# Forgetting attention and an expert layer: feeding the second stage group by group

## The chip, the cores and the metric

The kernel runs on one core of a Trainium2 chip. The core has a matrix engine (TensorE, shown as PE, with its weight loads as PEld), three engines for elementwise work (VectorE, shown as DVE; ScalarE, shown as ACT; GpSimd, shown as POOL) and a queue engine (SyncE, SP). Each works through its own instructions in a fixed order. Data moves between memory and the on-chip buffer by DMA; transfers are issued from SP, ACT and POOL and share 16 DMA engines. Matmul results land in PSUM, which has eight banks of 512 fp32 columns. The metric is the device time of the program in microseconds (us).

## The reference

Inputs: q, k, v of shape (8 batches, 8 heads, 576 positions, 64), forget gates f (8, 8, 576), and two weight matrices (512 x 2048 and 2048 x 512), all fp32.

```python
scores = (q @ k^T) / sqrt(64) + cum[..., :, None] - cum[..., None, :]   # cum = cumsum(log f)
scores = where(causal, -1e9, scores)          # a position sees itself and earlier ones
attn = softmax(scores)
x = (attn @ v)            # rearranged to (8*576 tokens, 512)
h = x @ w_in              # 4608 x 2048
out = (h - tanh(h)) @ w_out   # 4608 x 512
```

## The kernel before

A *group* is one batch entry: 8 heads of 576 positions. The 64 heads are one loop. `emit_group_dma` loads a group on POOL's queue, and `emit_group_transpose` turns q and k on PE (72 transposes of 128 columns) into QT and KT.

`emit_qk` makes the scores of a head, transposed: five tiles of up to 128 keys by the positions that see them (576, 448, 320, 192 and 64 wide). A tile is one matmul (two for the first, L172 and L174, since it is wider than a bank), an addition of the causal mask on its diagonal block by DVE (L179) and the exponential on ACT (L183). Tile 0 has a PSUM tile of its own of two banks (`ps_q0`), the others share two banks (`ps_qk`). The sum over keys needs no extra work: the values carry a column of ones, so `emit_av` gives 64 rows of weighted values and one row of sums in one PSUM tile (L199, L201). ACT copies that to `ot` (L207); SP sends the row of sums to `rsgt` (L208), and POOL sends the values, cast to fp16, into `xT` (L209), which holds x transposed: 4 blocks of 128 features (two heads each) by 4608 tokens.

`emit_group_finish` divides by the sums. DVE takes the reciprocal of a group's 8 rows (L214), ACT sends them to memory (L215), and then for each of 4 pairs of heads ACT's queue loads a broadcast `bcp`: one row to 64 partitions, the next to the other 64 (L218). DVE multiplies the block of `xT` with it (L221). `bcp` has 2 buffers.

The expert layer (MoE in the names) works in 9 units of 512 tokens. `emit_moe1` makes 16 pieces of the hidden layer: 4 matmuls (`hps`, L258), tanh on ACT (`th`, L262), the sum on DVE (`gt`, L265). `emit_moe2` makes 4 output tiles from 16 matmuls each (`ops`, L271), copied by ACT (`ost`, L274) and stored by SP (L276). A unit needs all four blocks of `xT` for its tokens, so unit u needs groups up to that of its last token: u for units 0 to 7, and group 7 for unit 8.

The order on each engine is drawn up when the program is built, by a planner of the Tile framework: it takes instructions by their place in the source as a priority, among those whose inputs and buffers are free by its own estimate of the times. So an instruction far down in the source may stand early in an engine's queue. In the source all eight `emit_group_finish` stand behind the head loop, then the attention's buffers are given back, then come the MoE's buffers, the weight loads and the units. A waiting instruction holds all behind it on its engine.

Of the kernel before, what the change touches and what calls it, by code (L numbers as in the profile page):

```python
# [1 line left out]

# [5 lines left out]
FP32 = mybir.dt.float32  # L9
BF16 = mybir.dt.bfloat16  # L10
FP16 = mybir.dt.float16
AF = mybir.ActivationFunctionType
ALU = mybir.AluOpType
# [5 lines left out]
def kernel(  # L19
# [10 lines left out]
    nc = tc.nc  # L30
    P = 128

    B, H, S, D = q.shape
    NH = B * H
    DM, DFF = moe_w_in.shape
# [3 lines left out]
    NJB = (S + P - 1) // P  # L39
# [3 lines left out]
    qscale = float(D) ** -0.5  # L43
    inv_qscale = float(D) ** 0.5
    NFT = DFF // P
    NCH = DM // P
    UW = 512
    NU = NT // UW
# [10 lines left out]
    qkt = tc.alloc_tile_pool(name="qkt", bufs=2)  # L59
    stg = tc.alloc_tile_pool(name="stg", bufs=2)  # L60
    vpl = tc.alloc_tile_pool(name="vpl", bufs=2 * H)
    aex = tc.alloc_tile_pool(name="aex", bufs=3 * NJB)
    fin = tc.alloc_tile_pool(name="fin", bufs=4)
    ps_tr = tc.alloc_tile_pool(name="ps_tr", bufs=2, space=bass.MemoryType.PSUM)
    ps_q0 = tc.alloc_tile_pool(name="ps_q0", bufs=1, space=bass.MemoryType.PSUM)
    ps_qk = tc.alloc_tile_pool(name="ps_qk", bufs=2, space=bass.MemoryType.PSUM)
    ps_av = tc.alloc_tile_pool(name="ps_av", bufs=1, space=bass.MemoryType.PSUM)

    xT = xtp.tile([P, NCH, NT], FP16)
    win = moe.tile([P, NCH, DFF], FP16)  # L70
    wout = moe.tile([P, NFT, DM], FP16)
# [20 lines left out]
    while sft < S:  # L92
        nc.vector.tensor_copy(out=dst[0:NH, 0:sft], in_=src[0:NH, 0:sft])
        nc.vector.tensor_tensor(out=dst[0:NH, sft:S], in0=src[0:NH, sft:S],
                                in1=src[0:NH, 0:S - sft], op=ALU.add)
# [9 lines left out]
    biasT = cst.tile([P, NJB, NH], FP32)  # L105
    for t in range(NJB):
        jn = JSZ[t]
# [5 lines left out]
    QTs, KTs, VAs, VTs, AEX, OTP, RSG, BCP = {}, {}, {}, {}, {}, {}, {}, {}  # L113
    rsdram = nc.dram_tensor("fox_rowsum", (NH, S), FP32).ap()
    rcdram = nc.dram_tensor("fox_rrowsum", (NH, S), FP32).ap()
# [43 lines left out]
    def emit_qk(h: int):  # L159
        g, hl = divmod(h, H)  # L160
        QT, KT = QTs[g], KTs[g]
        for t in range(NJB):
            j0 = t * P
            jn = JSZ[t]
            wid = S - j0
            if t == 0:
                ps = ps_q0.tile([P, 1024], FP32, tag="qk0")
            else:
                ps = ps_qk.tile([P, 512], FP32, tag="qk")
            lhsT = KT[0:D + 1, hl * S + j0: hl * S + j0 + jn]  # L170
            if t == 0:
                nc.tensor.matmul(out=ps[0:jn, 0:512],  # L172
                                 lhsT=lhsT, rhs=QT[0:D + 1, hl * S: hl * S + 512])
                nc.tensor.matmul(out=ps[0:jn, 512:S],  # L174
                                 lhsT=lhsT, rhs=QT[0:D + 1, hl * S + 512: hl * S + S])
            else:
                nc.tensor.matmul(out=ps[0:jn, 0:wid],  # L177
                                 lhsT=lhsT, rhs=QT[0:D + 1, hl * S + j0: hl * S + S])
            nc.vector.tensor_tensor(out=ps[0:jn, 0:jn], in0=ps[0:jn, 0:jn],  # L179
                                    in1=tri[0:jn, 0:jn], op=ALU.add)  # L180
            ae = aex.tile([P, S], FP16, tag="ae")
            AEX[(h, t)] = ae
            nc.scalar.activation(out=ae[0:jn, j0:S], in_=ps[0:jn, 0:wid], func=AF.Exp,  # L183
                                 bias=biasT[0:jn, t, h:h + 1], scale=qscale)

    def emit_av(h: int):
        g, hl = divmod(h, H)
        c = hl // 2
        upper = hl % 2
        assert H // 2 <= 4  # L190
        avp = ps_av.tile([P, 1024], FP32, tag="av")
        for t in range(NJB):
            j0 = t * P
            jn = JSZ[t]
            lhsT = (VTs[g][0:jn, hl, 0:D + 1] if t == NJB - 1
                    else VAs[h][0:jn, t, 0:D + 1])
            ae = AEX.pop((h, t))
            if j0 < 512:
                nc.tensor.matmul(out=avp[0:D + 1, j0:512], lhsT=lhsT, rhs=ae[0:jn, j0:512],  # L199
                                 start=(t == 0), stop=(t == NJB - 2))  # L200
            nc.tensor.matmul(out=avp[0:D + 1, 512:S], lhsT=lhsT, rhs=ae[0:jn, 512:S],  # L201
                             start=(t == 0), stop=(t == NJB - 1))
        m = H * S // P
        if hl == 0:
            RSG[g] = fin.tile([P, S], FP32, tag="rsg", name="rsgt")
        ot = fin.tile([P, S], FP32, tag="ot", bufs=6)
        nc.scalar.activation(out=ot[0:D + 1, :], in_=avp[0:D + 1, 0:S], func=AF.Copy)  # L207
        nc.sync.dma_start(out=RSG[g][hl:hl + 1, :], in_=ot[D:D + 1, 0:S])  # L208
        nc.gpsimd.dma_start(out=xT[upper * D:(upper + 1) * D, c, g * S:(g + 1) * S],  # L209
                            in_=ot[0:D, :])  # L210

    def emit_group_finish(g: int):
        rsg = RSG.pop(g)
        nc.vector.reciprocal(out=rsg[0:H, :], in_=rsg[0:H, :])  # L214
        nc.scalar.dma_start(out=rcdram[g * H:(g + 1) * H, :], in_=rsg[0:H, :])  # L215
        for c in range(H // 2):
            bcp = fin.tile([P, S], FP32, tag="bcp", bufs=2)
            nc.scalar.dma_start(  # L218
                out=bcp,
                in_=bass.AP(rcdram.tensor, (g * H + 2 * c) * S, [[S, 2], [0, D], [1, S]]))  # L220
            nc.vector.tensor_tensor(out=xT[:, c, g * S:(g + 1) * S],  # L221
                                    in0=xT[:, c, g * S:(g + 1) * S], in1=bcp, op=ALU.mult)

    pending = {}
    for hh in range(NH + 1):
        g, hl = divmod(hh, H)
        if hh == 0:
            pending[0] = emit_group_dma(0)
            emit_group_transpose(0, *pending.pop(0))
        if hh < NH:  # L230
            if hl == 1 and g + 1 < B:
                pending[g + 1] = emit_group_dma(g + 1)
            if hl == H - 2 and g + 1 < B:
                emit_group_transpose(g + 1, *pending.pop(g + 1))
            emit_qk(hh)
        if 1 <= hh <= NH:
            emit_av(hh - 1)
    for g in range(B):
        emit_group_finish(g)

    for p in (ps_av, ps_qk, ps_q0, ps_tr, fin, aex, vpl, stg, qkt):
        p.release()

    gtp = tc.alloc_tile_pool(name="gtp", bufs=2 * NFT)
    tmp = tc.alloc_tile_pool(name="tmp", bufs=2)
    ps_m1 = tc.alloc_tile_pool(name="ps_m1", bufs=2, space=bass.MemoryType.PSUM)
    ps_m2 = tc.alloc_tile_pool(name="ps_m2", bufs=2, space=bass.MemoryType.PSUM)

    nc.gpsimd.dma_start(out=win, in_=moe_w_in.rearrange("(c p) f -> p c f", p=P))
    nc.gpsimd.dma_start(out=wout, in_=moe_w_out.rearrange("(t p) e -> p t e", p=P))  # L250

    GT = {}

    def emit_moe1(u: int):
        for ft in range(NFT):
            hps = ps_m1.tile([P, UW], FP32, tag="m1")
            for ci in range(NCH):
                nc.tensor.matmul(out=hps, lhsT=win[:, ci, ft * P:(ft + 1) * P],  # L258
                                 rhs=xT[:, ci, u * UW:(u + 1) * UW],
                                 start=(ci == 0), stop=(ci == NCH - 1))  # L260
            th = tmp.tile([P, UW], FP32, tag="th")
            nc.scalar.activation(out=th, in_=hps, func=AF.Tanh, scale=-1.0)  # L262
            gt = gtp.tile([P, UW], FP16, tag="gt")
            GT[(u, ft)] = gt
            nc.vector.tensor_tensor(out=gt, in0=hps, in1=th, op=ALU.add)  # L265

    def emit_moe2(u: int):
        for m in range(UW // P):
            ops = ps_m2.tile([P, DM], FP32, tag="m2")
            for ft in range(NFT):  # L270
                nc.tensor.matmul(out=ops, lhsT=GT[(u, ft)][:, m * P:(m + 1) * P],  # L271
                                 rhs=wout[:, ft, :], start=(ft == 0), stop=(ft == NFT - 1))
            ost = tmp.tile([P, DM], FP32, tag="ost")
            nc.scalar.activation(out=ost, in_=ops, func=AF.Copy)  # L274
            r0 = u * UW + m * P
            nc.sync.dma_start(out=out[r0:r0 + P, :], in_=ost)  # L276

    for u in range(NU + 1):
        if u < NU:
            emit_moe1(u)  # L280
        if u > 0:
            emit_moe2(u - 1)

    for p in (ps_m2, ps_m1, tmp, gtp):
        p.release()


# [28 lines left out]
```

## Time and profile before

| | before |
|---|---|
| median of 6 runs | 700.12 us (699.83 to 700.81) |
| the profiled execution | 699.83 us, span 698.1 us |
| mean granted TensorE clock | 0.726 |
| instructions | 7647 |

The span runs from the first to the last instruction. Busy times count an engine's own work, without waits and without issuing DMAs. The clock is given as a share of full speed, 2.4 GHz; 0.50 is 1.2 GHz.

### The profile page before, as it was taken

How to read it: one execution, taken by the hardware profiler on the slowest of the kernel's cores; microseconds unless marked ns; L12 is line 12 of the kernel's file. 1: busy time of each engine (PE TensorE's matmuls, PEld its weight loads, DVE VectorE, ACT ScalarE, POOL GpSimd, SP SyncE). 2: the span in 40 equal slices, each digit the busy share in tenths (PEclk: the TensorE clock that was granted, in tenths of full speed). 3: DMA queues.
4: the chain of work that ended last, by engine and by line, in shares of the span. 5: the costliest groups of instructions: out<-in, count | busy, mean ns of one | idle time of the engine just before them, and what ended most of it. 6: DMA issues, size and time to landing. Idle time of an engine off the chain costs nothing.

```text
span 698.1 us, 7647 instructions
## 1 busy us (share of the span) xinstructions
PE 531.4 (76%) x2693; PEld 277.5 (40%) x2693; DVE 283.5 (41%) x611; ACT 291.0 (42%) x567; POOL 127.4 (18%) x244
## 2 busy tenths in 40 slices
PE   2899626465866757867845646299999999999997
PEld 1566313333443434534423322034444444444443
DVE  6547322514524624624624234244533524425330
ACT  1558422344444435444544532144433534434331
POOL 6647502332332332222001000000000000000000
PEclk9759655555555555555565558589999999999999
DMA  9999993993494594334111220100011010010111
GB/s 98 104 103 93 117 166 52 151 110 57 42 113 68 48 97 67 31 52 67 15 51 40 45 55 23 46 31 31 15 46 45 31 46 30 31 62 15 46 46 76
DMA packets 131479, 42.97 MB, mean 62 GB/s; under 512 B 115888, under 2 KB 122096, under 8 KB 131440
## 3 DMA queue, kind: packets, MB, share of 16 engines
q0 software_dynamic: 119712, 23.08, 43.3%
q1 hardware_dynamic: 7440, 9.81, 3.9%
q10 hardware_dynamic: 4288, 9.59, 3.9%
q8 instruction: 21, 0.34, 0.2%
q14 instruction: 18, 0.15, 0.1%
HBM read 46.28 MB, written 9.58 MB: 80 GB/s over the span
## 4 chain that ended last, share of the span: by engine, by line
PE 39%; DMA 14%; DVE 3%; ACT 2%; issue 1%; DVEq 0%; ACTq 0%
PE hps L258 18%; PE ops L271 17%; DMA bcp<-fox_rrowsum 13%; DVE rsgt L214 2%; PE ps L177 1%; ACT ae L183 1%; PE avp L199 1%; DVE ps L179 1%; PE tq L150 0%; PE tk L155 0%; PE ps L172 0%; DVE xT L221 0%; ACT ot L207 0%; PE avp L201 0%; DMA xT<-ot 0%
## 5 line engine op out<-in xcount | busy, mean ns | idle before, releaser
L183 ACT ACTIVATE ae<-ps,biasT 128x576 f16<-128x576 f32 (+4 forms) x320 | 148.8, 521 | 215.1 <-DVE ps L179 214.5
L258 PE MATMUL hps<-xT,win 128*128 128x512 f16 x576 | 143.3, 390 | 23.4 <-DVE gt L265 23.4
L177 PE MATMUL ps<-QT,KT 65*128 65x448 bf16 (+3 forms) x256 | 86.1, 387 | 97.1 <-ACT ae L183 95.1
L265 DVE TENSOR_TENSOR gt<-hps,th 128x512 f16<-128x512 f32 x144 | 99.2, 690 | 131.2 <-ACT th L262 131.2
L271 PE MATMUL ops<-wout,gt 128*128 128x512 f16 x576 | 138.2, 382 | 0.0
L262 ACT ACTIVATE th<-hps 128x512 f32<-128x512 f32 x144 | 86.0, 597 | 108.0 <-PE hps L258 94.8
L179 DVE TENSOR_TENSOR ps<-ps,tri 128x128 f32<-128x128 f32 (+1 forms) x320 | 79.4, 278 | 89.9 <-PE ps L177 54.7
L199 PE MATMUL avp<-ae,va 128*65 128x512 f16 (+3 forms) x256 | 98.3, 435 | 8.8 <-ACT ot L207 7.5
L258 PEld LDWEIGHTS <-win 128*128 128x128 f16 x576 | 56.6, 99 | 99.2 <-issue 41.2
L221 DVE TENSOR_TENSOR xT<-xT,bcp 128x576 f16<-128x576 f16 x32 | 24.3, 759 | 151.6 <-DMA bcp<-fox_rrowsum 147.8
L271 PEld LDWEIGHTS <-gt 128*128 128x128 f16 x576 | 56.7, 98 | 69.3 <-issue 2.2
L177 PEld LDWEIGHTS <-KT 65*128 65x128 bf16 (+1 forms) x256 | 32.1, 132 | 126.9 <-issue 123.7
L209 POOL DMA_DIRECT2D xT<-ot x64 | 34.2, 535 | 164.1 <-ACT ot L207 156.2
L133 POOL DMA_DIRECT2D va<-in_v_dram x64 | 49.7, 779 | 56.5 <-issue 39.1
L201 PE MATMUL avp<-ae,va 128*65 128x64 f16 x256 | 58.8, 248 | 0.0
L155 PE MATMUL tk<-idbf,ksb 128*65 128x128 bf16 x288 | 44.6, 291 | 14.3 <-DVE KT L157 9.0
L199 PEld LDWEIGHTS <-va 128*65 128x65 f16 x256 | 40.4, 158 | 31.8 <-issue 23.1
L274 ACT ACTIVATE ost<-ops 128x512 f32<-128x512 f32 x36 | 21.4, 596 | 66.8 <-PE ops L271 66.8
L201 PEld LDWEIGHTS <-va 128*65 128x65 f16 x256 | 40.4, 158 | 17.7 <-issue 15.2
L150 PE MATMUL tq<-idbf,qsb 128*64 128x128 bf16 x288 | 42.2, 293 | 5.7 <-DVE QT L152 4.4
L207 ACT ACTIVATE ot<-avp 65x576 f32<-65x576 f32 x64 | 41.1, 642 | 11.9 <-PE avp L201 11.9
L155 PEld LDWEIGHTS <-ksb 128*65 128x65 bf16 x288 | 31.1, 156 | 25.6 <-issue 15.9
(40 smaller groups left out, 267.7 us busy)
## 6 DMA issues: line engine op xcount, KB each, us to landing
bcp<-fox_rrowsum ACTq DMA_DIRECT2D x32, 288.0 KB
out_dram<-ost SPq DMA_DIRECT2D x36, 256.0 KB
qsb<-in_q_dram POOLq DMA_DIRECT2D x8, 576.0 KB, 7.6
ksb<-in_k_dram POOLq DMA_DIRECT2D x8, 576.0 KB, 10.5
xT<-ot POOLq DMA_DIRECT2D x64, 72.0 KB, 4.8
va<-in_v_dram POOLq DMA_DIRECT2D x64, 64.0 KB, 6.0
win<-in_moe_w_in_dram POOLq DMA_DIRECT2D x1, 2048.0 KB, 39.3
wout<-in_moe_w_out_dram POOLq DMA_DIRECT2D x1, 2048.0 KB, 15.9
```

Of the source, the lines that this page charges most:

```text
L133: nc.gpsimd.dma_start(out=va[:, :, 0:D], in_=vf[g * H + hl, 0:JTOP, :].rearrange("(n p) d -> p n d", p=P))
L150: nc.tensor.transpose(out=tq[0:D, t * P:(t + 1) * P], in_=qsb[:, c0 + t, :], identity=idbf)
L155: nc.tensor.transpose(out=tk[0:D + 1, t * P:(t + 1) * P], in_=ksb[:, c0 + t, :], identity=idbf)
L177: nc.tensor.matmul(out=ps[0:jn, 0:wid], lhsT=lhsT, rhs=QT[0:D + 1, hl * S + j0: hl * S + S])
L179: nc.vector.tensor_tensor(out=ps[0:jn, 0:jn], in0=ps[0:jn, 0:jn], in1=tri[0:jn, 0:jn], op=ALU.add)
L183: nc.scalar.activation(out=ae[0:jn, j0:S], in_=ps[0:jn, 0:wid], func=AF.Exp, bias=biasT[0:jn, t, h:h + 1], scale=qscale)
L199: nc.tensor.matmul(out=avp[0:D + 1, j0:512], lhsT=lhsT, rhs=ae[0:jn, j0:512], start=(t == 0), stop=(t == NJB - 2))
L201: nc.tensor.matmul(out=avp[0:D + 1, 512:S], lhsT=lhsT, rhs=ae[0:jn, 512:S], start=(t == 0), stop=(t == NJB - 1))
L258: nc.tensor.matmul(out=hps, lhsT=win[:, ci, ft * P:(ft + 1) * P], rhs=xT[:, ci, u * UW:(u + 1) * UW], start=(ci == 0), stop=(ci == NCH - 1))
L262: nc.scalar.activation(out=th, in_=hps, func=AF.Tanh, scale=-1.0)
L265: nc.vector.tensor_tensor(out=gt, in0=hps, in1=th, op=ALU.add)
L271: nc.tensor.matmul(out=ops, lhsT=GT[(u, ft)][:, m * P:(m + 1) * P], rhs=wout[:, ft, :], start=(ft == 0), stop=(ft == NFT - 1))
```

## The change

The source order is rearranged, and some buffers change size.

- `emit_group_finish(g)` and the units that its tokens complete now stand in the head loop, three heads after the last `emit_av` of the group; queued pieces of units (one `emit_moe1` of 4 matmuls, or one `emit_moe2` of 16) are emitted three to a step of the loop. The loop has 24 more steps for what is left.
- The MoE has its own buffers from the start: two PSUM banks `ps_m1` for `hps`; `ops` shares `ps_tr` with the transposes; 16 `gt` buffers instead of 32. For that the scores lose `ps_q0`: the last 64 columns of tile 0 become a tile of their own in `ps_qk`, with an exponential of their own. `aex` goes from 15 to 10 buffers, `ot` from 6 to 5.
- The weights are loaded at the second head, behind the loads of group 1.
- Each broadcast load is two transfers, one for each half of the partitions.
- `ost` is copied by DVE instead of ACT.

```diff
-    aex = tc.alloc_tile_pool(name="aex", bufs=3 * NJB)
+    aex = tc.alloc_tile_pool(name="aex", bufs=2 * NJB)
-    ps_q0 = tc.alloc_tile_pool(name="ps_q0", bufs=1, space=bass.MemoryType.PSUM)
     ps_qk = tc.alloc_tile_pool(name="ps_qk", bufs=2, space=bass.MemoryType.PSUM)
+    ps_m1 = tc.alloc_tile_pool(name="ps_m1", bufs=2, space=bass.MemoryType.PSUM)
...
-            if t == 0:
-                ps = ps_q0.tile([P, 1024], FP32, tag="qk0")
-            else:
-                ps = ps_qk.tile([P, 512], FP32, tag="qk")
+            ps = ps_qk.tile([P, 512], FP32, tag="qk")
...
-                nc.tensor.matmul(out=ps[0:jn, 512:S],
+                psb = ps_qk.tile([P, 512], FP32, tag="qk")
+                nc.tensor.matmul(out=psb[0:jn, 0:S - 512],
                                  lhsT=lhsT, rhs=QT[0:D + 1, hl * S + 512: hl * S + S])
+                nc.scalar.activation(out=ae[0:jn, 512:S], in_=psb[0:jn, 0:S - 512],
+                                     func=AF.Exp, bias=biasT[0:jn, t, h:h + 1], scale=qscale)
+                wid = 512
...
-        ot = fin.tile([P, S], FP32, tag="ot", bufs=6)
+        ot = fin.tile([P, S], FP32, tag="ot", bufs=5)
...
             bcp = fin.tile([P, S], FP32, tag="bcp", bufs=2)
-            nc.scalar.dma_start(
-                out=bcp,
-                in_=bass.AP(rcdram.tensor, (g * H + 2 * c) * S, [[S, 2], [0, D], [1, S]]))
+            for u2 in range(2):
+                nc.scalar.dma_start(
+                    out=bcp[u2 * D:(u2 + 1) * D, :],
+                    in_=bass.AP(rcdram.tensor, (g * H + 2 * c + u2) * S, [[0, D], [1, S]]))
...
+    gtp = tc.alloc_tile_pool(name="gtp", bufs=NFT)
+    tmp2 = tc.alloc_tile_pool(name="tmp2", bufs=2)
+    GT = {}
+    moeq = deque()
...
+    def emit_moe2(u, m):
+        def run():
+            ops = ps_tr.tile([P, DM], FP32, tag="tr")
+            for ft in range(NFT):
+                nc.tensor.matmul(out=ops, lhsT=GT[(u, ft)][:, m * P:(m + 1) * P],
+                                 rhs=wout[:, ft, :], start=(ft == 0), stop=(ft == NFT - 1))
+            ost = tmp2.tile([P, DM], FP32, tag="ost")
+            nc.vector.tensor_copy(out=ost, in_=ops)
+            r0 = u * UW + m * P
+            nc.sync.dma_start(out=out[r0:r0 + P, :], in_=ost)
+        return run
+
+    nxt_u = [0]
+
+    def push_ready_moe(gdone: int):
+        while nxt_u[0] < NU and ((nxt_u[0] * UW + UW - 1) // S) <= gdone:
+            u = nxt_u[0]
+            for ft in range(NFT):
+                moeq.append(emit_moe1(u, ft))
+            for m in range(UW // P):
+                moeq.append(emit_moe2(u, m))
+            nxt_u[0] += 1
...
-    for hh in range(NH + 1):
+    for hh in range(NH + 3 * H):
...
                 pending[g + 1] = emit_group_dma(g + 1)
+                if g == 0:
+                    nc.gpsimd.dma_start(out=win, in_=moe_w_in.rearrange("(c p) f -> p c f", p=P))
+                    nc.gpsimd.dma_start(out=wout, in_=moe_w_out.rearrange("(t p) e -> p t e", p=P))
...
-    for g in range(B):
-        emit_group_finish(g)
...
+        if hh >= H + 3 and (hh - 3) % H == 0 and (hh - 3) // H - 1 < B:
+            emit_group_finish((hh - 3) // H - 1)
+            push_ready_moe((hh - 3) // H - 1)
+        for _ in range(3):
+            if moeq:
+                moeq.popleft()()
```

`emit_moe1(u, ft)` in the new form is one piece of the old one, with `hps` from `ps_m1` as before.

## Rows read from the trace of the kernel before

**Rows 1.** The page's busy time by engine: us, share of the span, instructions.
```profile
PE 531.4 (76%) x2693; PEld 277.5 (40%) x2693; DVE 283.5 (41%) x611; ACT 291.0 (42%) x567; POOL 127.4 (18%) x244
```
**Rows 2.** The page's chain that ended last, shares of the span by line.
```profile
PE hps L258 18%; PE ops L271 17%; DMA bcp<-fox_rrowsum 13%; DVE rsgt L214 2%; PE ps L177 1%; ACT ae L183 1%; PE avp L199 1%; DVE ps L179 1%; PE tq L150 0%; PE tk L155 0%; PE ps L172 0%; DVE xT L221 0%; ACT ot L207 0%; PE avp L201 0%; DMA xT<-ot 0%
```
**Rows 3.** Single lines' instructions: ns min/median/max, first and last start in us, shapes.
```profile
L207 ACT ACTIVATE ot<-avp x64: 634/640/647, 27.7 to 413.7; 65x576 f32<-65x576 f32 x64
L258 PE MATMUL hps<-xT,win x576: 376/377/634, 345.4 to 670.8; 128*128 128x512 f16 x192
L214 DVE RECIPROCAL rsgt<-rsgt x8: 3728/3740/3742, 68.7 to 420.1; 8x576 f32<-8x576 f32 x8
```
**Rows 4.** Stretches: length, engines' busy us (instructions), then clock, DMA share, GB/s.
```profile
core 0: us, PE busy (x) PEld busy (x) DVE busy (x) ACT busy (x) POOL busy (x), PEclk, DMA share, GB/s
40.00:52.00 12.00, 12.00 (x73) 7.72 (x72) 5.54 (x15) 5.99 (x12) 3.05 (x4) 0.50 1.68 112
52.00:72.00 20.00, 18.07 (x167) 12.02 (x165) 15.27 (x37) 14.63 (x31) 15.01 (x30) 0.97 1.41 99
60.00:68.00 8.00, 8.00 (x82) 5.59 (x81) 6.61 (x18) 6.16 (x14) 6.79 (x10) 1.00 1.58 113
344.00:352.00 8.00, 7.81 (x35) 3.67 (x36) 3.06 (x12) 5.36 (x12) 0.52 (x1) 0.63 0.13 22
512.19:540.24 28.05, 28.05 (x130) 12.42 (x128) 11.06 (x16) 11.83 (x20) 0.00 (x0) 1.00 0.10 37
```
**Rows 5.** Waits: who waited for whom, us in total, times, the longest.
```profile
DVE xT L221 <- DMA bcp<-fox_rrowsum: 147.8, 31, 13.5
```
**Rows 6.** Order of events around 310 us: start, us, instruction, idle time before it.
```profile
309.49 0.76 DVE L221 TENSOR_TENSOR xT<-xT,bcp 128x576 f16<-128x576 f16 x1 [6.34 <-DMA bcp<-fox_rrowsum]
...
310.50 1.05 ACT L183 ACTIVATE ae<-ps,biasT 128x448 f16<-128x448 f32 x2 [6.20 <-DVE ps L179]
311.18 0.63 PE L177 MATMUL ps<-QT,KT 65*128 65x192 bf16 x2 [5.42 <-ACT ae L183]
```
**Rows 7.** The page's DMA queue (packets, MB, share) and issues (count, KB, us to landing).
```profile
q10 hardware_dynamic: 4288, 9.59, 3.9%
...
win<-in_moe_w_in_dram POOLq DMA_DIRECT2D x1, 2048.0 KB, 39.3
wout<-in_moe_w_out_dram POOLq DMA_DIRECT2D x1, 2048.0 KB, 15.9
```
**Rows 8.** Order of events in the last group's division, 440 to 456 us.
```profile
442.00 0.49 ACTq L218 DMA_DIRECT2D bcp<-fox_rrowsum  x1
...
447.07 0.76 DVE L221 TENSOR_TENSOR xT<-xT,bcp 128x576 f16<-128x576 f16 x1 [3.16 <-DMA bcp<-fox_rrowsum]
452.94 0.76 DVE L221 TENSOR_TENSOR xT<-xT,bcp 128x576 f16<-128x576 f16 x1 [5.10 <-DMA bcp<-fox_rrowsum]
```
**Rows 9.** Order of events at the end of the span, ACT.
```profile
694.37 0.60 ACT L274 ACTIVATE ost<-ops 128x512 f32<-128x512 f32 x1 [2.86 <-PE ops L271]
```
**Rows 10.** Groups of ACT instructions by shape: count, busy us, mean ns, idle before.
```profile
L274 ACT ACTIVATE ost<-ops 128x512 f32<-128x512 f32 x36 | 21.4, 596 | 66.8 <-PE ops L271 66.8
L183 ACT ACTIVATE ae<-ps,biasT 64x64 f16<-64x64 f32 x64 | 19.4, 304 | 3.4 <-DVE ps L179 3.1
...
L183 ACT ACT_TABLE_LOAD x1 | 1.3, 1283 | 0.0
```
**Rows 11.** Line L209 (`xT<-ot`): issue ns, first and last start; then issue to landing.
```profile
L209 POOL DMA_DIRECT2D xT<-ot x64: 515/532/630, 35.9 to 414.7; - x64
...
DMA to landing us min/median/max: 2.2/4.8/39.4
```
**Rows 12.** Order of events on ACT around 53 us.
```profile
52.87 0.65 ACT L207 ACTIVATE ot<-avp 65x576 f32<-65x576 f32 x1 [0.94 <-PE avp L201]
```
**Rows 13.** Chain that ended last, in order of time, within one unit.
```profile
514.57 1.79 PE hps L258 x8
516.35 0.65 PE ops L271 x3
```

More of the change, by code (lines that the diff above doesn't have):

```diff
@@ L2 @@
+from collections import deque
 from contextlib import ExitStack
@@ L165, in emit_qk @@
             wid = S - j0
-            if t == 0:
-                ps = ps_q0.tile([P, 1024], FP32, tag="qk0")
-            else:
-                ps = ps_qk.tile([P, 512], FP32, tag="qk")
+            ps = ps_qk.tile([P, 512], FP32, tag="qk")
             lhsT = KT[0:D + 1, hl * S + j0: hl * S + j0 + jn]
+            ae = aex.tile([P, S], FP16, tag="ae")
+            AEX[(h, t)] = ae
             if t == 0:
@@ L180, in emit_qk @@
                                     in1=tri[0:jn, 0:jn], op=ALU.add)
-            ae = aex.tile([P, S], FP16, tag="ae")
-            AEX[(h, t)] = ae
-            nc.scalar.activation(out=ae[0:jn, j0:S], in_=ps[0:jn, 0:wid], func=AF.Exp,
+            nc.scalar.activation(out=ae[0:jn, j0:j0 + wid], in_=ps[0:jn, 0:wid], func=AF.Exp,
                                  bias=biasT[0:jn, t, h:h + 1], scale=qscale)
@@ L217, in emit_group_finish, with emit_moe1, run @@
             bcp = fin.tile([P, S], FP32, tag="bcp", bufs=2)
-            nc.scalar.dma_start(
-                out=bcp,
-                in_=bass.AP(rcdram.tensor, (g * H + 2 * c) * S, [[S, 2], [0, D], [1, S]]))
+            for u2 in range(2):
+                nc.scalar.dma_start(
+                    out=bcp[u2 * D:(u2 + 1) * D, :],
+                    in_=bass.AP(rcdram.tensor, (g * H + 2 * c + u2) * S, [[0, D], [1, S]]))
             nc.vector.tensor_tensor(out=xT[:, c, g * S:(g + 1) * S],
                                     in0=xT[:, c, g * S:(g + 1) * S], in1=bcp, op=ALU.mult)
+    gtp = tc.alloc_tile_pool(name="gtp", bufs=NFT)
+    tmp2 = tc.alloc_tile_pool(name="tmp2", bufs=2)
+    GT = {}
+    moeq = deque()
+    def emit_moe1(u, ft):
+        def run():
+            hps = ps_m1.tile([P, UW], FP32, tag="m1")
+            for ci in range(NCH):
+                nc.tensor.matmul(out=hps, lhsT=win[:, ci, ft * P:(ft + 1) * P],
+                                 rhs=xT[:, ci, u * UW:(u + 1) * UW],
+                                 start=(ci == 0), stop=(ci == NCH - 1))
+            th = tmp2.tile([P, UW], FP32, tag="th")
+            nc.scalar.activation(out=th, in_=hps, func=AF.Tanh, scale=-1.0)
+            gt = gtp.tile([P, UW], FP16, tag="gt")
+            GT[(u, ft)] = gt
+            nc.vector.tensor_tensor(out=gt, in0=hps, in1=th, op=ALU.add)
+        return run
+    def emit_moe2(u, m):
+        def run():
+            ops = ps_tr.tile([P, DM], FP32, tag="tr")
[6 more added lines that the diff above has]
+            nc.sync.dma_start(out=out[r0:r0 + P, :], in_=ost)
+        return run
+    nxt_u = [0]
[7 more added lines that the diff above has]
+            nxt_u[0] += 1
     pending = {}
-    for hh in range(NH + 1):
+    for hh in range(NH + 3 * H):
         g, hl = divmod(hh, H)
@@ L237 @@
             emit_av(hh - 1)
-    for g in range(B):
-        emit_group_finish(g)
[L241 to L284, printed above, removed]
+        if hh >= H + 3 and (hh - 3) % H == 0 and (hh - 3) // H - 1 < B:
[4 more added lines that the diff above has]
+                moeq.popleft()()
+    while moeq:
+        moeq.popleft()()
+    for p in (tmp2, gtp, ps_av, ps_m1, ps_qk, ps_tr, fin, aex, vpl, stg, qkt):
         p.release()
```

## The prediction

> **What bounds the kernel now.** The engine totals say that none is full over the run: PE is busy 76% of the span, DVE and ACT 41% and 42% [rows 1]. So I read the chain that ended last: PE on the two MoE matmuls, and 13% of the span on the transfer `bcp<-fox_rrowsum` [rows 2]. The run has two stages. The last weighted output of a head (`ot`) starts at 413.7 us, the first at 27.7, while the MoE's first matmul comes at 345.4 and its last at 670.8 [rows 3]. In a unit of the second stage PE is busy 28.05 of 28.05 us at granted clock 1.00 (2.4 GHz) [rows 4]: it is at its limit there, and the only gain is to begin sooner. In the first stage the waits name the cause: DVE stood idle 147.8 us in 31 waits for `bcp` to land [rows 5]. The order of events shows that this is one stall: at 309.49 DVE ends 6.34 us of waiting and multiplies; the mask additions stood behind it in its queue; at 310.50 ACT can take the exponentials, idle for 6.20 us; at 311.18 PE, idle for 5.42 us, gets a score bank back [rows 6]. So a slow transfer that a low-priority multiply waits for stops the attention, some 4.8 us at a time.
>
> Why is `bcp` slow? Its queue moved 4288 packets in 3.9% of 16 engines' 698.1 us [rows 7], that is 436 us / 4288 = 0.102 us each. A transfer has 128 rows, so 13.0 us of one engine's time. In the last group two successive multiplies wait for their transfers and start at 447.07 and 452.94, so one transfer lands each 5.87 us [rows 8]: 13.0 / 5.87 = 2.2 engines at work, of 16. Four of them take some 24 us of each group.
>
> **The change, part by part.** (1) Each `bcp` load becomes two transfers of 64 rows, whose outermost dimension is 64 instead of 2. The 2.2 engines fit the 2; if the rows now spread over all 16, a half needs 64 x 0.102 / 16 = 0.4 us of each engine. No row shows a landing for it. Bounds: below, 0.4 us; above, the 10.9 us from issue to multiply of a whole one in the last group, 442.00 to 452.94 [rows 8]. Nearest is the store of the last output tile, also 128 rows of about 2 KB: ACT ends it at 694.97 and the span ends at 698.1 [rows 9], so it lands within 3.1 us. I take 2 to 3 us. DVE reached the multiplies late enough to wait 4.8 us on average of a pace of 5.9, so at 3 us most of the 147.8 us go. ACT pays 32 more issues at 0.49 us [rows 8], 16 us over the run, 2 us a group, beside idle time.
>
> The Trainium skill ("DMA: Bandwidth & Descriptors", section "Rules for kernel authors") says that an outermost dimension smaller than 16, such as a leading zero-stride broadcast, confines a DMA to that many engines: 2 before, 16 after, and the 2.2 of this trace agrees. The same table also speaks against the edit: two transfers to disjoint partition halves are not worth doing, since both share the same engines. By that line alone nothing is won, which is the second rival and its 690; by the other line the sum stands.
>
> (2) MoE units (512 tokens) get memory of their own from the start, so unit u can run as soon as its group is finished: 0 to 6 beside the heads of groups 1 to 7, only 7 and 8 after them. Cost on PE: in the stretch 60 to 68 at clock 1.00, 82 attention matmuls kept it busy 8.00 us, 0.0976 each; in 40 to 52 at 0.50, 73 took 12.00 us, 0.164 each [rows 4]. A group has 8 x 15 matmuls in the heads and 72 transposes, 192: 18.7 us at the full clock, 31.6 at the half. A unit has 128 matmuls and took 28.05 us at clock 1.00 [rows 4], so 56.1 at half. A group with its unit thus needs 46.8 us of PE at the full clock, 87.7 at the half.
>
> DVE and ACT are no bound. ACT loses 36 `ost` copies (21.4 us) and gains 64 short exponentials, since the 576-wide one is split: at the 304 ns of the 64-wide form, 19.5 us less what the shorter main one saves. DVE gains the 36 copies, no row of its own for them: at ACT's 596 ns [rows 10] 21.5 us, at twice that 43. So from the totals [rows 1] some 289 and 305 us (at most 327) of some 550. Exp and Tanh already alternate on ACT from 345.4 to 414 [rows 3] with one table load ahead of all the exponentials and none after it [rows 10], so mixing them costs nothing there.
>
> What is not hidden: the scores of a head now take six tiles from two banks, where tile 0 had a bank pair of its own. Between two uses of a bank lie one matmul, one addition and one exponential, while MoE pieces and weighted values can fill PE. I cost it inside the efficiency of the next sentence, with nothing (46.8) and a third more (63) as its ends. In 52 to 72, without a `bcp` wait, PE was busy 18.07 of 20 us [rows 4], 0.90; 46.8 / 0.90 = 52.0, and the 3.7 us reciprocal [rows 3], in which the mask additions behind it wait, makes 55.7 us an interval.
>
> (3) The weights move to the second step of the head loop, on POOL's queue ahead of the `xT<-ot` copies. In the trace one such copy landed 39.4 us after its issue, against a median of 4.8 [rows 11], and `win` itself took 39.3, `wout` 15.9 [rows 7]. Now both stand in front, and after five heads (`ot` has 5 buffers, before 6) ACT and so PE must wait. Head 5 comes at 52.87 [rows 12]; the first copy, issued at 35.9 [rows 11], could land as late as 36 + 55 = 91. Bounds 0 and 38 us, once; I take 20, the middle, since part of the 39.3 was shared with `bcp`.
>
> (4) The tail. After the last head: reciprocal 3.7, row sums out 3.1 at most, two rounds of two broadcasts (0.98 issue + 3.1) and two multiplies of 0.76: 16.5 us, less what is left of unit 6; I take 8 of 0 to 16.5. Then units 7 and 8. With 16 instead of 32 `gt` buffers a unit's first layer no longer runs beside the second layer of the unit before; the old chain shows 8 `hps` with 3 `ops` in 2.44 us [rows 13], where those three fill the gap. So 16 pieces at 1.22 and 64 matmuls at 0.219: 33.5 each, 67 in all (56 if the overlap stays).
>
> Sum. The first reciprocal starts at 68.7 [rows 3], so group 0 is done at about 70. 70 + 20 + 7 x 55.7 + 8 + 67 + 3 (the last store) = 558 us of span; outside the span lie 699.83 - 698.1 = 1.7 us. That is **560 us**, against 699.83 for the profiled execution, which is 0.3 below the median of six.
>
> **Rivals.**
> *Little overlap.* The planner fills PE with the MoE only where its estimates leave it idle, and two score banks or in-order queues keep the two works apart. An attention group without the waits: (413.7 - 70) / 7 = 49.1, less 147.8 / 8 = 18.5, so 30.6. Then 70 + 20 + 7 x 30.6 + 16.5 + 9 x 33.5 + 3 + 1.7 = 627 us. For it: the PE order now keeps attention dense and the MoE late. Against: heads leave PE idle and all buffers are free.
>
> *The halves are no faster.* The waits stay, 18.5 us a group, uncovered: 560 + 7 x 18.5 = 690; half covered, 625. For it: the same bytes and queue. Against: 2.2 engines of 16.
>
> *Slower: PE stays at 1.2 GHz.* In 40 to 52 PE was busy 12.00 of 12 us and the clock stayed at 0.50 [rows 4]; being busy with attention is not enough. Were it so for the mixture, 87.7 us an interval give 70 + 20 + 7 x 87.7 + 8 + 67 + 3 + 1.7 = 784. It decides from 75.8 us an interval ((700.1 - 169.7) / 7, all terms of the sum but the intervals), about two thirds of the time at half clock. Against it: the few MoE matmuls among heads came with clock 0.63 in 344 to 352, and the steady MoE with 1.00 [rows 4], and two thirds of an interval's PE columns are MoE (128 x 512 against 8 x 3200 + 72 x 128).
>
> *Better.* All intervals at 46.8, weights hidden, tail overlapped: 70 + 328 + 56 + 5 = 459.
>
> **Chances.** Forecast (480 to 610) 0.70; little overlap 0.15; halves no faster 0.06; PE at half clock 0.06; below 480, 0.03. The range 480 to 650 takes in the forecast, most of the first rival and the better half of the second; the forecast's own is 500 to 610, from intervals of 47 to 63. 0.2%, 1.4 us, is about what separates a change from none here. Slower 0.06 is the clock rival; same 0.01 from the gap between it and the second; faster 0.93.
>
> **What would show it.** Right: DVE's wait for `bcp` falls from 147.8 below 30 us; first `hps` at 75 to 110, not 345.4; the `ot` of the last head at 460 to 500 with two units behind it; mean granted clock over 0.80 instead of 0.726; a gap in `ot` before 90 for the weights. Wrong: `bcp` waits over 100 us; four or more units after the last head; intervals over 65 us at clock near 0.5, or DVE and ACT queues waiting in turn while PE is under 75% busy.

## The result, and the profile after

The changed kernel takes **500.52 us** (median of 8 runs, 497.90 to 501.17) against 700.11 us (16 runs of the kernel before): a ratio of 0.7145, 95% interval 0.7134 to 0.7155. The forecast was 560 us with a range of 480 to 650. The direction and the mechanism were right; the gain was 200 us instead of 140, since the time between two groups was put too long.

The page of the profile after: busy time, the granted clock in 40 slices of 12.5 us, and the chain that ended last by line. These answer to [rows 1, 2].

```profile
span 498.7 us, 7727 instructions
...
PE 449.1 (90%) x2693; PEld 231.8 (46%) x2693; DVE 304.1 (61%) x647; ACT 276.7 (55%) x595; POOL 127.9 (26%) x244
...
PEclk9958556769999999999999999999999999979999
...
PE hps L236 26%; PE ops L250 23%; PE ps L181 7%; PE avp L201 6%; DMA ksb<-in_k_dram 4%; PE tq L151 4%; DMA bcp<-fox_rrowsum 3%; PE tk L156 3%; DMA win<-in_moe_w_in_dram 3%; PE avp L203 3%; PE ps L172 2%; POOL va L134 2%; DVE xT L224 1%; DMA va<-in_v_dram 1%; DMA rsgt<-ot 1%
```

PE went from 76% of the span to 90%. It is also busy fewer microseconds (449 instead of 531) for the same matmuls, since most of the heads' work now runs at 2.4 GHz. The broadcast fell from 13% of a longer chain to 3%. Four stretches of the changed kernel say where PE still stands; the columns are those of [rows 4].

```profile
50.00:100.00 50.00, 30.67 (x170) 17.42 (x170) 19.80 (x46) 20.46 (x44) 21.15 (x38) 0.60 1.49 139
125.00:375.00 250.00, 249.43 (x1622) 130.76 (x1621) 176.75 (x381) 165.31 (x366) 64.83 (x125) 1.00 0.64 83
423.00:436.00 13.00, 9.05 (x40) 3.84 (x40) 4.89 (x7) 0.63 (x2) 0.00 (x0) 0.99 0.54 174
436.00:495.00 59.00, 57.58 (x248) 24.28 (x247) 26.96 (x40) 18.38 (x31) 0.00 (x0) 0.94 0.09 32
```

For 250 us PE is full at the full clock. It is short of work at 50 to 100, while DMA loads the weights and the next groups, and for a few microseconds in the last group's division.

The heads' outputs, the first layer's matmuls and the reciprocals (one line's instructions each) answer to [rows 3], the waits to [rows 5].

```profile
L209 ACT ACTIVATE ot<-avp x64: 633/646/663, 25.4 to 413.9; 65x576 f32<-65x576 f32 x64
L236 PE MATMUL hps<-xT,win x576: 376/379/634, 88.2 to 484.7; 128*128 128x512 f16 x192
L216 DVE RECIPROCAL rsgt<-rsgt x8: 3729/3730/3742, 73.4 to 418.6; 8x576 f32<-8x576 f32 x8
```

```profile
DVE xT L224 <- DMA bcp<-fox_rrowsum: 19.6, 13, 4.9
...
PE hps L236 <- DVE xT L224: 9.8, 5, 5.1
```

The last head is done at 413.9 us, where it was done before (413.7); but by then seven of nine units are nearly through, whose first matmul came at 345.4 before and comes at 88.2 now. DVE's 147.8 us of waiting for `bcp` are 19.6. The heads did not get faster as a stage: the time that they wasted now holds the MoE.

The last group's division, on the chain in order of time, against [rows 8]:

```profile
423.87 0.45 ACTq L221
424.36 3.33 DMA bcp<-fox_rrowsum
427.80 0.77 DVE xT L224
...
429.87 0.48 ACTq L221
430.38 3.59 DMA bcp<-fox_rrowsum
434.09 0.77 DVE xT L224
```

From the first issue to the multiply a broadcast takes 3.9 us. The one issued at 442.00 took 10.9, but that one had another in flight ahead of it, multiplied at 447.07 [rows 8]; the fairer comparison is the last half column here, issued behind others at 429.87 and multiplied at 434.09, 4.2 us later.

### The profile page after: what moved, and what is told of

It reads as the page before. It is cut to its first block, busy times and chain, and to the rows that moved or that the text cites. A ratio compares the mean times of both kernels' runs of the same rounds, so it can differ in the third digit from the quotient of the medians.

```text
span 498.7 us, 7727 instructions
## 1 busy us (share of the span) xinstructions
PE 449.1 (90%) x2693; PEld 231.8 (46%) x2693; DVE 304.1 (61%) x647; ACT 276.7 (55%) x595; POOL 127.9 (26%) x244
## 3 DMA queue, kind: packets, MB, share of 16 engines
q0 software_dynamic: 119712, 23.08, 60.5%
## 4 chain that ended last, share of the span: by engine, by line
PE 73%; DMA 13%; issue 5%; POOL 4%; DVE 3%; ACT 1%; ACTq 0%; DVEq 0%; POOLq 0%
PE hps L236 26%; PE ops L250 23%; PE ps L181 7%; PE avp L201 6%; DMA ksb<-in_k_dram 4%; PE tq L151 4%; DMA bcp<-fox_rrowsum 3%; PE tk L156 3%; DMA win<-in_moe_w_in_dram 3%; PE avp L203 3%; PE ps L172 2%; POOL va L134 2%; DVE xT L224 1%; DMA va<-in_v_dram 1%; DMA rsgt<-ot 1%
## 5 line engine op out<-in xcount | busy, mean ns | idle before, releaser
L185 ACT ACTIVATE ae<-ps,biasT 128x512 f16<-128x512 f32 (+4 forms) x320 | 155.3, 516 | 53.4 <-DVE ps L183 52.2
L236 PE MATMUL hps<-xT,win 128*128 128x512 f16 x576 | 158.4, 390 | 11.9 <-DVE xT L224 9.8
L201 PE MATMUL avp<-ae,va 128*65 128x512 f16 (+3 forms) x256 | 72.8, 326 | 8.5 <-ACT ot L209 8.4
L134 POOL DMA_DIRECT2D va<-in_v_dram x64 | 49.6, 776 | 118.5 <-issue 76.9
L181 PE MATMUL ps<-QT,KT 65*128 65x448 bf16 (+3 forms) x256 | 74.1, 294 | 6.3 <-ACT ae L185 3.3
L177 ACT ACTIVATE ae<-psb,biasT 128x64 f16<-128x64 f32 x64 | 19.9, 311 | 68.0 <-PE psb L175 55.0
L209 ACT ACTIVATE ot<-avp 65x576 f32<-65x576 f32 x64 | 41.2, 644 | 13.4 <-DMA xT<-ot 7.2
L203 PE MATMUL avp<-ae,va 128*65 128x64 f16 x256 | 47.0, 202 | 0.0
L253 DVE COPY ost<-ops 128x512 f32<-128x512 f32 x36 | 24.3, 676 | 30.5 <-PE ops L250 30.5
L181 PEld LDWEIGHTS <-KT 65*128 65x128 bf16 (+1 forms) x256 | 26.3, 104 | 32.4 <-issue 19.6
L201 PEld LDWEIGHTS <-va 128*65 128x65 f16 x256 | 29.8, 117 | 22.6 <-issue 8.5
L203 PEld LDWEIGHTS <-va 128*65 128x65 f16 x256 | 30.2, 120 | 17.9 <-issue 12.6
L224 DVE TENSOR_TENSOR xT<-xT,bcp 128x576 f16<-128x576 f16 x32 | 24.1, 752 | 20.5 <-DMA bcp<-fox_rrowsum 19.6
L151 PE MATMUL tq<-idbf,qsb 128*64 128x128 bf16 x288 | 32.4, 243 | 0.6 <-DMA qsb<-in_q_dram 0.6
L156 PE MATMUL tk<-idbf,ksb 128*65 128x128 bf16 x288 | 29.3, 238 | 2.8 <-POOL va L137 2.7
## 6 DMA issues: line engine op xcount, KB each, us to landing
win<-in_moe_w_in_dram POOLq DMA_DIRECT2D x1, 2048.0 KB, 14.9
wout<-in_moe_w_out_dram POOLq DMA_DIRECT2D x1, 2048.0 KB, 24.3
```

What stands on the lines that cost most here:

```text
L134: nc.gpsimd.dma_start(out=va[:, :, 0:D], in_=vf[g * H + hl, 0:JTOP, :].rearrange("(n p) d -> p n d", p=P))
L151: nc.tensor.transpose(out=tq[0:D, t * P:(t + 1) * P], in_=qsb[:, c0 + t, :], identity=idbf)
L156: nc.tensor.transpose(out=tk[0:D + 1, t * P:(t + 1) * P], in_=ksb[:, c0 + t, :], identity=idbf)
L181: nc.tensor.matmul(out=ps[0:jn, 0:wid], lhsT=lhsT, rhs=QT[0:D + 1, hl * S + j0: hl * S + S])
L185: nc.scalar.activation(out=ae[0:jn, j0:j0 + wid], in_=ps[0:jn, 0:wid], func=AF.Exp, bias=biasT[0:jn, t, h:h + 1], scale=qscale)
```

## The experiments

All times are medians with the ratio to the kernel before, run on the same chip. "Interval" is the time from the start of `ot` of the 8th head to that of the 64th, over seven groups.

| run | time, us | ratio (95%) | interval, us |
|---|---|---|---|
| before | 700.1 | 1 | 50.7 |
| changed kernel | 500.5 | 0.7145 (0.7134 to 0.7155) | 49.6 |
| 1 split only | 574.2 | 0.8232 (0.8196 to 0.8268) | 35.6 |
| 2 changed, broadcast unsplit | 664.9 | 0.9534 (0.9498 to 0.9569) | 70.8 |
| 3 changed, 61 and 3 rows | 808.4 | 1.1574 (1.1529 to 1.1620) | 88.3 |
| 4 changed, MoE behind the heads | 609.9 | 0.8727 (0.8698 to 0.8755) | 46.4 |
| 5 split only, two score banks | 614.2 | 0.8796 (0.8761 to 0.8831) | 41.3 |
| 6 changed, two pieces a step | 524.6 | 0.7492 (0.7449 to 0.7535) | 49.3 |
| 7 changed, later weights | 499.6 | 0.7151 (0.7120 to 0.7182) | 50.8 |
| 8 changed, a third load | 507.3 | 0.7247 (0.7204 to 0.7289) | 49.5 |
| 9 changed, four `bcp` buffers | 494.7 | 0.7063 (0.7030 to 0.7097) | 49.6 |
| 10 both 9 and 7 | 496.7 | 0.7090 (0.7036 to 0.7143) | 50.6 |

The starts of `ot` of the 8th head are 59.06 (before), 66.39 (changed), and 59.07, 65.53, 65.52, 64.63, 60.59, 65.95, 62.16, 74.78, 66.45 and 63.14 in runs 1 to 10.

**1. The split alone.**

```diff
-            nc.scalar.dma_start(
-                out=bcp,
-                in_=bass.AP(rcdram.tensor, (g * H + 2 * c) * S, [[S, 2], [0, D], [1, S]]))
+            for u2 in range(2):
+                nc.scalar.dma_start(
+                    out=bcp[u2 * D:(u2 + 1) * D, :],
+                    in_=bass.AP(rcdram.tensor, (g * H + 2 * c + u2) * S, [[0, D], [1, S]]))
```

> The kernel before with one edit: each broadcast load is two transfers of 64 rows. Theory (two DMA engines at work instead of sixteen made the 147.8 us of waits): the waits of DVE for bcp fall below 30 us, a group of heads takes 31 to 36 us instead of 49, the last head comes at 290 to 340 instead of 413.7, the MoE stage stays about 244 us long, time 550 to 600 us. Rival (the halves share the same engines and are no faster; all the gain is from the new order of the MoE): waits stay near 148 us, 690 to 705 us.

574 us. This edit of a few lines gives 126 us by itself. The multiply's group (its busy time, mean, and idle time before it with the releaser) and the heads' outputs:

```profile
L222 DVE TENSOR_TENSOR xT<-xT,bcp 128x576 f16<-128x576 f16 x32 | 23.8, 747 | 29.6 <-DMA bcp<-fox_rrowsum 29.6
```

```profile
L207 ACT ACTIVATE ot<-avp x64: 635/641/647, 27.4 to 308.5; 65x576 f32<-65x576 f32 x64
```

The wait falls by 118 us, and the last head comes 105 us sooner, at 308.5. The theory holds.

**2. The changed kernel with the broadcast in one transfer again** (the reverse of the same edit).

> The changed kernel with the broadcast loaded in one transfer of 128 rows again. Theory: two engines serve it, one lands each 5.9 us, DVE waits 80 to 150 us in all, intervals of 55 to 62 us instead of 49, time 540 to 600 us. Rival (the MoE work beside the heads hides the transfer, the split was not needed): waits under 60 us, 500 to 515 us.

665 us, beyond both expectations. So the new order without the split is worth 35 us. Two of its waits:

```profile
DVE xT L223 <- DMA bcp<-fox_rrowsum: 173.0, 32, 7.2
...
PE hps L235 <- DVE xT L223: 76.6, 20, 5.9
```

DVE waits longer than before (173.0 against 147.8). I put this down to the division's place in the source: it now ranks ahead of the heads that follow it, so its multiplies come earlier in the queue; no run tests that alone. And the MoE did not hide the wait: its matmuls wait 76.6 us for those multiplies, and its own additions stand in the same DVE queue. I had expected the MoE's matmuls to cover most of the stall; an interval of 70.8 is the 49.6 and 21 more, nearly all of the 4 x 5.9 us that four transfers take.

**3. An odd number of rows.**

```diff
             for u2 in range(2):
-                nc.scalar.dma_start(
-                    out=bcp[u2 * D:(u2 + 1) * D, :],
-                    in_=bass.AP(rcdram.tensor, (g * H + 2 * c + u2) * S, [[0, D], [1, S]]))
+                for d0, dn in ((0, 61), (61, 3)):
+                    nc.scalar.dma_start(
+                        out=bcp[u2 * D + d0:u2 * D + d0 + dn, :],
+                        in_=bass.AP(rcdram.tensor, (g * H + 2 * c + u2) * S, [[0, dn], [1, S]]))
```

> The changed kernel with each half of the broadcast cut into transfers of 61 and 3 rows: the same bytes in twice as many transfers as in the changed kernel, but 61 is a prime. Theory (the number of engines follows the outermost dimension): the 61 rows run on one engine, about 61 x 0.102 = 6.2 us each, two of them one after the other for a column, so a column lands each 12 us, worse than unsplit: waits of DVE 200 us or more, 600 to 700 us. Rival (more, smaller transfers are what helps): 500 to 520 us.

808 us, slower than the kernel before by 16%. Two successive multiplies by `bcp` on DVE, late in the run:

```profile
649.77 0.76 DVE L225 TENSOR_TENSOR xT<-xT,bcp 128x576 f16<-128x576 f16 x1 [7.11 <-DMA bcp<-fox_rrowsum]
...
661.83 0.76 DVE L225 TENSOR_TENSOR xT<-xT,bcp 128x576 f16<-128x576 f16 x1 [8.56 <-DMA bcp<-fox_rrowsum]
```

They stand 12.06 us apart, as one engine would give (2 x 61 rows of 0.102 us are 12.4). Same bytes, more transfers than in the changed kernel: an outermost dimension of 2 gave 5.9 us a column, 61 gave 12, 64 gave waits that nearly vanish. The number of rows decides over the engines, not the number of transfers.

The profile page's packet counts for that queue point the same way. First the changed kernel, then this run; the kernel before and run 2 have 4288 [rows 7].

```profile
q10 hardware_dynamic: 5248, 9.59, 6.4%
```

```profile
q10 hardware_dynamic: 4480, 9.59, 3.4%
```

The bytes are the same, so the 960 and 192 packets above 4288 are very small ones. They come out if each engine that takes part in a transfer adds one packet: 64 x 16 - 32 x 2 = 960, and 64 x (1 + 3) - 32 x 2 = 192. That an engine adds one is an inference from this fit; with it the counts give 2 engines for the whole broadcast, 16 for a half, 1 for 61 rows and 3 for 3 rows.

The time that I expected was too low for the reason of run 2: of 48 us of transfer for a group 39 lie bare, an interval of 88.3 against 49.6.

**4. The MoE behind the heads.**

```diff
-        for _ in range(3):
-            if moeq:
-                moeq.popleft()()
```

> The changed kernel with its buffers, weights and divisions as they are, but the pieces of the MoE stand behind the head loop in the source, so that the planner puts 127 hps and 86 ops matmuls ahead of the last weighted value instead of 440 and 385. Theory (the place in the source makes the overlap): last head at 320 to 370, then some 939 matmuls or 206 to 240 us, time 540 to 590 us, PE near full only behind the heads. Rival (memory of its own is enough, the order is worth nothing): 495 to 515 us.

610 us, 20 above what I expected, and the last head comes at 389.2, not at 320 to 370. The overlap is made by the place in the source, as the theory said; but this is 36 us more than run 1, which has no overlap either, and the interval is 46.4 with only 213 MoE matmuls beside the heads. Something else in the change makes the heads slower. Run 5 tests the score banks.

**5. Split only, six score tiles over two banks.**

```diff
-            if t == 0:
-                ps = ps_q0.tile([P, 1024], FP32, tag="qk0")
-            else:
-                ps = ps_qk.tile([P, 512], FP32, tag="qk")
+            ps = ps_qk.tile([P, 512], FP32, tag="qk")
...
+                psb = ps_qk.tile([P, 512], FP32, tag="qk")
...
```

> The kernel of the first experiment (before, with split broadcasts; 574 us) with the scores of a head as six tiles over the two banks of ps_qk, as in the changed kernel, and the other two banks unused. Theory (heads without MoE work between them feel the lost banks, which would explain why the run with the MoE behind the heads took 610 us, 36 more than split only): PE waits longer for exponentials, interval 38 to 41 us instead of 35.6, time 590 to 615 us. Rival (the banks are hidden, the 36 us come from the MoE pieces that sit among the heads and from 16 gt buffers): 570 to 582 us.

614 us, 40 more than run 1. The heads' outputs, and PE's wait for the exponentials that give a bank back, here and then in run 1:

```profile
L208 ACT ACTIVATE ot<-avp x64: 633/639/647, 25.2 to 349.4; 65x576 f32<-65x576 f32 x64
```

```profile
PE ps L180 <- ACT ae L184: 40.6, 31, 3.7
...
PE ps L171 <- ACT ae L184: 10.2, 11, 4.5
...
PE ps L180 <- ACT ae L176: 8.1, 11, 2.5
```

```profile
PE ps L177 <- ACT ae L183: 32.7, 16, 4.3
```

58.9 us of such waits instead of 32.7, and a last head at 349.4 instead of 308.5. The lost banks (with the split exponential, which this run can't tell from them) cost the heads 5.7 us a group when nothing else fills PE. Waits are only part of it: from the 8th head's output to the last one's PE is also busy longer with the same work, at a lower granted clock: 223.30 us at 0.61, against 203.21 us at 0.65 in run 1 (its line stands with the rivals below).

```profile
60.59:349.40 288.81, 223.30 (x1262) 126.52 (x1263) 153.11 (x373) 177.45 (x392) 88.11 (x166) 0.61 0.81 89
```

**6. Two pieces a step.**

```diff
-        for _ in range(3):
+        for _ in range(2):
```

> The changed kernel with two pieces of the MoE emitted per step of the head loop instead of three: 355 hps and 330 ops matmuls ahead of the last weighted value instead of 440 and 385. Theory (PE is full from 125 us on, so where its work stands no longer matters as long as there is enough beside the heads): the intervals get shorter and the tail longer by the same, 495 to 506 us. Rival (each matmul moved behind the heads costs its 0.22 us): 140 x 0.22 = 31 us more, 525 to 535 us.

524.6 us, at the edge of the rival's 525 to 535: 24 us more, where the 140 matmuls moved behind the heads take 31. From the last head to the end it takes 112.4 us instead of 84.8, and the last head comes only 3 us sooner, at 410.9. The mean interval hardly shrinks (49.3), but it hides two kinds: the last three intervals are 46.9, 44.7 and 41.5 us (49.1, 49.0 and 43.8 in the changed kernel), as the theory wanted, while the two between 164 and 278 us are 60.5 and 53.3. One stretch of 50 us in them:

```profile
225.00:275.00 50.00, 39.16 (x246) 20.47 (x245) 29.67 (x66) 29.30 (x66) 15.77 (x29) 0.86 0.90 74
```

PE is busy 39 of 50 us here, where it was full in the changed kernel, and the clock is at half for part of it. With runs 4 and 5 this is a series: with two score banks, 8, 213, 685 and 825 MoE matmuls beside the heads give intervals of 41.3, 46.4, 49.3 and 49.6 us. The first 205 cost 36 us, the next 612 only 23, where 612 matmuls behind the heads would cost 134 at 0.219 each. The heads' own chain leaves that time on PE. That is why the overlap is worth so much. (Run 5 differs from the other three in the rest of the change too, and each run has an order of its own from the planner, so the steps of the series are not exact prices.)

**7. Later weights.**

```diff
-                if g == 0:
-                    nc.gpsimd.dma_start(out=win, in_=moe_w_in.rearrange("(c p) f -> p c f", p=P))
-                    nc.gpsimd.dma_start(out=wout, in_=moe_w_out.rearrange("(t p) e -> p t e", p=P))
+            if hh == H:
+                nc.gpsimd.dma_start(out=win, in_=moe_w_in.rearrange("(c p) f -> p c f", p=P))
+            if hh == H + 2:
+                nc.gpsimd.dma_start(out=wout, in_=moe_w_out.rearrange("(t p) e -> p t e", p=P))
```

They were issued at 36.3 and 67.6 us instead of 35.4 and 36.1.

> The changed kernel with the load of win one group later in the source and that of wout two heads behind it. On POOL the planner then puts one xT copy ahead of win and 25 more instructions between win and wout. Theory (copies of the first heads wait behind both weights, 15 us of standstill at 45.9 to 60.8): the standstill halves, ACT's wait for the xT copy (7.2 us) goes, the PE work behind it stays, time 490 to 496 us. Rival (the loads of group 1 and 2 fill the queue anyway, the standstill has another cause): 499 to 503 us.

499.6 us: nothing, as the rival said. ACT's wait for the `xT` copy is gone, but the slow stretch has only moved: the outputs of the 8th to 12th head start at 62, 70, 79, 85 and 98 us (66, 71, 80, 88 and 98 in the changed kernel).

**8. A third load of 2 MB.**

```diff
+                    nc.gpsimd.dma_start(out=xT[:, :, 4 * S:4 * S + DFF],
+                                        in_=moe_w_in.rearrange("(c p) f -> p c f", p=P))
```

> The changed kernel with a third load of 2 MB (moe_w_in once more, into the part of xT that groups 4 to 7 overwrite long after) behind the two weights. Theory (the first 100 us are bound by what the loads move, so the standstill is the traffic and not the place of one transfer; moving the weights therefore won nothing): 2 MB at the 140 GB/s of 25 to 75 us are 14 us more, 508 to 518 us. Rival (there is slack in the loads, the standstill comes from the order of the instructions): 498 to 503 us.

507.3 us, 7 more: outside the rival's interval, half of what I expected. The output of the sixth head, first in the changed kernel, then here:

```profile
60.82 0.65 ACT L209 ACTIVATE ot<-avp 65x576 f32<-65x576 f32 x1 [7.16 <-DMA xT<-ot]
```

```profile
69.89 0.65 ACT L209 ACTIVATE ot<-avp 65x576 f32<-65x576 f32 x1 [11.42 <-DMA xT<-ot]
```

The standstill ends 9 us later for 2 MB more. So the copies do wait for the loads ahead of them. With run 7 this says that what has to be loaded counts in the first 100 us, and that moving one load does not make it smaller; how much of that time the loads bound in all is not shown.

**9. Four `bcp` buffers**, paid for with two `rsgt` instead of four.

```diff
-            RSG[g] = fin.tile([P, S], FP32, tag="rsg", name="rsgt")
+            RSG[g] = fin.tile([P, S], FP32, tag="rsg", name="rsgt", bufs=2)
...
-            bcp = fin.tile([P, S], FP32, tag="bcp", bufs=2)
+            bcp = fin.tile([P, S], FP32, tag="bcp", bufs=4)
```

> The changed kernel with four bcp buffers instead of two, paid for with two rsgt buffers instead of four. Theory (in the last group the second pair of broadcasts waits for the first multiplies, 427.8 to 434.1, while PE has only 6 us of idle time there): 3 to 6 us less, 494 to 498 us; DVE's waits for bcp fall from 19.6 to about 10 us. Rival (the planner's order, not the buffer, sets when they are issued): 499 to 502 us.

494.7 us, the best version: its interval lies wholly below that of the changed kernel. But DVE's waits for `bcp` stay (19.3 us). The gain is in the last group. The last head comes at 413.9 as in the changed kernel, and the span ends 5.7 us sooner. The first matmul after the division starts at 432.0 instead of 434.9, and the granted clock behind the division stays at 1.00; the stretch behind it, to be read against the one from 436 to 495 above:

```profile
436.00:493.00 57.00, 52.59 (x239) 22.71 (x237) 25.82 (x38) 17.10 (x29) 0.00 (x0) 1.00 0.10 38
```

**10. Four buffers and later weights**, the edits of runs 9 and 7 together.

> Four bcp buffers (494.7 us) together with the later weights (499.6 us). Theory (the later weights only move the standstill): 492 to 497 us, not below the four buffers alone. Rival (with the queue of broadcasts shorter, the earlier transposes of group 1 count): 485 to 491 us.

496.7 us; its interval overlaps that of run 9. The later weights add nothing here either.

## Why the prediction came out as it did

*What bounded the kernel* was read rightly. The waits for `bcp` were the price: run 1 changes nothing but that transfer and gains 126 us. The reckoning of 2.2 engines from packets and landings is borne out by the three sizes of runs 1 to 3 (12 us a column on one engine, 5.9 on two) and by the packet counts under run 3. Of the signs that it named, four came: waits of 19.6 us, a first `hps` at 88.2, a mean clock of 0.93, and a gap in `ot` before 90 (45.9 to 60.8). One did not: the last head is at 413.9 instead of 460 to 500, for the first two terms below.

The Trainium skill ("DMA: Bandwidth & Descriptors", section "Rules for kernel authors") states that an outermost dimension below 16 confines the whole DMA to at most that many engines, and the 5.9 us a column for a dimension of 2 agrees. The same table has the rule against splitting into partition halves. Here the measurement decides for the first: the halves are worth 126 us alone and 164 us in the changed kernel (664.9 to 500.5), since the whole transfer was not on all engines.

*The sum* was 558 us of span and 498.7 came out, by three terms.

- Start: 70 + 20 us, against 66.4 to the eighth head. The 70 was drawn at the first reciprocal, although group 1's heads run beside it; the eighth head of the kernel before was at 59.1. And of the 20 us for the weights 7.3 were paid: `win` and `wout`, issued at 35.4 and 36.1 us, landed in 14.9 and 24.3 us instead of 39.3 and 15.9 [rows 7], so both were there at about 60 us, and the slowest `xT` copy took 23.5 us, not 39.4 [rows 11]. No slow broadcast was in their way any more: in run 1, which issues `win` at 84.1 us where the kernel before does at 83.7, the split alone brings it from 39.3 to 19.2. 23.6 us too much. The lines of the DMA issues, and of the copies from issue to landing:

```profile
win<-in_moe_w_in_dram POOLq DMA_DIRECT2D x1, 2048.0 KB, 14.9
wout<-in_moe_w_out_dram POOLq DMA_DIRECT2D x1, 2048.0 KB, 24.3
```

```profile
DMA to landing us min/median/max: 2.2/2.4/23.5
```

- Intervals: 7 x 55.7, against 7 x 49.6. **This is the term that was mis-sized.** Five of the seven intervals, 124 to 370 us, are 49.0 to 50.1 us, four of them with exactly the 320 matmuls of a group and a unit; the first, with the loads, is 57.6, and the last, which has no next group to transpose, 43.8. PE's own 46.8 us for those matmuls were thus 2.2 too few, and the 8.9 us on top, the efficiency of 0.90 and the 3.7 of the reciprocal, had nothing to answer to: from 125 to 375 us PE is busy 249.43 of 250 us. In the stretch that the 0.90 came from, PE had attention alone to do; with pieces of the MoE in its queue it has something to run while DVE is in the reciprocal. 42.3 us too much in all.
- Tail: 8 + 67 + 3, against 84.8 from the last head to the end. The division took 21 us to the last multiply (413.9 to 434.9), of which PE worked for most of the time on what was left of unit 6. The two units took 60.0 us (434.9 to 494.9), not 67: with 16 `gt` buffers the second layer of the same unit fills the gaps of the first (18 of its 64 matmuls in the case of unit 7), which the step had denied. 6.8 us too little: the division, put at 8, took 13 us more, the units 7 less.

*The rivals.* Little overlap was wrong for this order. Run 4, without the loop that spreads the pieces, comes to 610 us, and the 627 worked out for it is near only by luck: the intervals are 46.4 us and not 30.6, 110 us more in seven, while the start is 25 us shorter (64.6 instead of 90) and the tail 102 us (218.7 instead of 321). "The halves are no faster" is refuted by runs 1 to 3; its price was too low: 130 us on top of the forecast, where run 2 takes 164 more than the changed kernel. That 690 and 664.9 lie near each other comes from the forecast's own 60 us too many. The clock rival is refuted: the mixture holds 2.4 GHz from 125 to 425 us. Heads alone did not, as the heads of groups 1 to 7 in run 1 show (the columns as above):

```profile
59.00:308.00 249.00, 203.21 (x1260) 123.56 (x1259) 142.15 (x370) 157.30 (x335) 92.22 (x172) 0.65 0.98 104
```

*The lost score banks*, costed inside the efficiency with ends of 0 and 16 us an interval, cost 5.7 without the MoE (run 5). With it they are not to be seen: PE is full, and its waits for exponentials that give a bank back come to 6.1 us in all, against 58.9 in run 5. No run gives the changed kernel its banks back.

Still open: what part of the first 100 us each load has (runs 7 and 8 change two of many), and why two pieces a step leave PE idle at 175 to 275 us (run 6).

## What to carry to other kernels

Work out from packets and landings how many DMA engines a slow transfer uses before moving work around it: here the outermost dimension of an access pattern was worth more than the whole rearrangement, and the rearrangement was worth 35 us without it and 74 with it. The two gave 126 and 35 us alone and 200 together, so each has to be tested alone and with the other. Filler work did not hide the stall here (run 2), where it stood in the queue that stalled.

## What the runs showed of the hardware

The price of an outermost dimension: 2 rows gave 5.9 us a column, 61 with 3 gave 12.06, and 64 a landing within 3.9 us of the issue.

Behind a short idle stretch of PE a second price can stand: in the changed kernel PE is idle for 4 of the 13 us from 423 to 436, in the last division, and the granted clock is 0.86 between 425 and 450 us. In run 9, whose first matmul after the division comes 3 us sooner, it is 1.00 there.

A full PE was seen at either level of the clock: with attention alone at 0.50 from 40 to 52 us and at 1.00 from 60 to 68 [rows 4]. Run 1's heads, with PE busy 82% of the time, had a mean clock of 0.65, and the mixture with the MoE, with PE busy 99%, ran at 1.00 from 125 to 425 us. The two differ in the work and in the busy share, so no run here tells which of them made the difference.
